# A new order for 1,687 hand-listed steps of an attention and expert kernel, fewer warm matmuls and one tiny activation

## The chip, the cores and the metric

The kernel runs on one core of a Trainium2 chip. The metric is device time in microseconds (us) of one execution, as the median of three runs. Its engines are TensorE (PE in the profile, its weight loads PEld), VectorE (DVE), ScalarE (ACT), GpSimd (POOL) and SyncE (SP), which here only issues transfers. Each works off its own queue in order, and semaphores tie them together.

## What is computed

Two stages follow each other: attention through 32 packed queries, in which softmax is taken twice, and then a feed-forward layer with a SiLU between two products.

```python
# q, k, v: (8, 8, 576, 64); p: (8, 8, 32, 64); w_in: (512, 2048); w_out: (2048, 512), all float32
def sm_attn(qq, kk, vv):
    s = scale * np.matmul(qq, kk.transpose(0, 1, 3, 2))
    a = np.exp(s - np.max(s, axis=-1, keepdims=True))
    return np.matmul(a / (np.sum(a, axis=-1, keepdims=True) + 1e-09), vv)
p_packed = sm_attn(p, k, v)
x = sm_attn(q, p_packed, p_packed)       # then (tokens, 512): 4608 x 512
h = x @ w_in
out = (h * (1.0 / (1.0 + np.exp(-h)))) @ w_out
```

## The kernel before

The program is a list of steps, `ORDER` (lines 56 to 123), that the last loop (lines 897 to 899) works off: a name, then numbers. Each step issues its instructions on one or two engines, and for TensorE, VectorE, ScalarE and SyncE an engine's queue is exactly the order in which the list names its steps. A queue that waits for a semaphore holds all behind it. So the list is the schedule, and a step late in one queue can hold three others.

The work falls into eight batches of 576 tokens, in two halves of 288 each. The steps that the text speaks of:

- Weights, in 20 chunks: `wf` loads a chunk (SP), `ws` scales (ACT), `wc`, `wz`, `wi` clip, sign and shift (DVE), `wj` joins (DVE, for some chunks POOL), `wu` and `wl` make an upper and a lower part (ACT, DVE). They split each float32 weight in two parts that TensorE multiplies at its faster float32 rate.
- Attention of batch b, `a` and a letter, then b and the half: `aS` or `as` scores (PE), `ac`/`aC` copies (ACT or DVE), `am`/`aM` maxima (DVE), `ax`/`aX` exponentials (ACT, the Exp table), `at` transposes (PE for batch 0, else DVE), `ay` spreads (for batches 1 to 7 small transfers issued by SP, line 383, eight for a half), `aa` the packed product (PE), `an`, `aj` scaling and copy (DVE) around `ai`, a transpose (PE), `aB` and `aU` transposes of batch 0 (PE), `aN`, `aD`, `aE`, `aV` differences, sums, shares and block transposes (DVE), `aH` and `aL` upper and lower part (ACT, DVE). `k`, `v`, `q` load a batch's inputs into two buffers that are used in turn.
- `pf`, `pp`, `pu`, `pl`: fetch a quarter of w_in, multiply it with the packed values (PE), and split the product (ACT, DVE).
- The feed-forward layer in units. Units 0 to 31 (batches 0 and 1): `h` (PE, line 611), `g` (ACT, the Silu table), `l` (DVE), `o` (PE, line 669). Units from 36 on: `B` (PE, line 611), `G` and `N` (ACT, Silu), `I` (three adds on POOL), `F` (ACT), `L` (DVE), `O` (PE, line 669). An `O` multiplies with sums of pairs of weights, which `S` loads (SP, line 740) into four buffers in turn. `E` and `Y` add up and store a half or the remaining rows (DVE, ACT, then SP).
- `r`, `R`, `ru`, `rl`, `rk`, `T` make and store those sums of weights during the first third.
- `W` (line 206) issues so many matmuls whose result nobody reads; `X0` and `X1` (line 187) are activations of one column, which make the compiler load the Exp or the Silu table there.

Two pairs of PSUM banks, `ps_two`, are used in turn by `W`, `h`, `B`, `pp` and the attention of batches 1 to 7 (line 200): a step that takes a pair waits until the readers of the step two turns earlier are done. All `W` steps share one pair that is taken once (lines 208 and 209), and the first two `pp` steps share another (lines 555 to 558).

Of the kernel before, what the change touches and what calls it, by code (L numbers as in the profile page):

```python
# [66 lines left out]
aH1.1 ac2.0 pl5 aL1.1 o6 o7 e7.0 r0 e7.1 h8 g8 ws13 l8 h9 g9 o8 ws14 wz12 wi12 wj12 as2.1 ac2.1 l9 am2 wc14 pp6 pu6  # L67
h10 pl6 g10 l10 X0 wc13 o9 v2 wz14 wi14 R0 h11 wz13 wi13 ax2.0 ax2.1 o10 g11 h12 wf15 wj13 l11 o11 at2.0 at2.1 wf17
ru0 rl0 rk0 ws15 ay2 g12 wc15 l12 h13 g13 h14 l13 pp7 o12 r1 pu7 g14 wz15 wj14 wi15 wu14 wj15 wu15 pl7 l14 wl15 o13
wl14 h16 wf16 ws17 wc17 q2 h15 g15 l15 R1 wz17 wi17 ru1 rl1 rk1 o14 o15 r2 g16 l16 e15.0 e15.1 ws16 h17 ar2 h18 g17  # L70
wj17 o16 h19 l17 wf18 g18 wc16 wz16 R2 ru2 l18 o17 wi16 wj16 pp8 rl2 r3 g19 pu8 l19 pl8 aa2 o18 h20 an2 X1 ai2 wf19
ws18 wc18 wz18 rk2 o19 wi18 aj2 g20 l20 aS2.1 x1 b0 aT2.1 wj18 pp9 ws19 wc19 x3 wu18 wl18 h21 pu9 pl9 g21 l21 x2 wz19
wi19 o20 h22 g22 l22 aM2.1 aN2.1 R3 h24 h23 wj19 wu19 wl19 ru3 rl3 rk3 X0 o21 r4 R4 o22 T0 T3 g23 l23 o23 g24 l24 h25
h26 e23.0 ru4 rl4 rk4 e23.1 g25 l25 r5 o24 pp10 g26 l26 aS2.0 o25 aT2.0 pu10 pl10 aX2.1 h27 aM2.0 aN2.0 aX2.0 aD2.0 X1
b1 aE2.0 T1 T2 h28 k3 o26 R5 ru5 rl5 rk5 T5 g27 l27 h29 T4 aV2.0 aH2.0 g28 r6 R6 l28 o27 g29 l29 o28 h31 aD2.1 aL2.0
h30 ru6 rl6 rk6 T6 r7 o29 g30 R7 l30 aE2.1 aV2.1 v3 g31 o30 aH2.1 ru7 X0 l31 rl7 o31 rk7 e31.0 e31.1 pp11 Z0. pp12 Z1.
F32 L32 O32 aL2.1 pf13 S36 pu11 T7 pl11 as3.1 pu12 F33 pl12 S37 as3.0 ac3.0 L33 O33 ac3.1 F34 am3 F35 ax3.0 B36 L34
G36 S39 I36 B37 G37 L35 N37 N36 O34 ax3.1 S38 pp13 pu13 O35 B38 pl13 pf14 at3.0 F36 I37 Y0 L36 F37 at3.1 G38 I38 L37
B39 N38 N39 ay3.0 O36 ar3 B40 G39 I39 F38 L38 pp14 pu14 q3 N40 O37 G40 O38 I40 B41 F39 L39 G41 pl14 F40 I41 L40 B42
G42 X1 O39 S40 O40 N41 F41 N42 ay3.1 B43 N43 I42 F42 L41 S41 aa3 G43 O41 X0 an3 L42 ai3 aj3 B44 S42 N44 G44 aS3.0 O42  # L80
B45 S44 I43 aT3.0 aM3.0 B46 F43 L43 I44 F44 N45 L44 G45 I45 S45 S43 aN3.0 O43 S46 pf15 E2.0 G46 F45 L45 N46 B47 O44
G47 N47 S47 pp15 I46 aS3.1 F46 L46 pu15 pl15 aT3.1 aX3.0 aD3.0 pf16 I47 O45 F47 O46 L47 B49 aE3.0 X1 k4 S49 N49 G49
S48 I49 B48 G48 pp16 pu16 aM3.1 O47 I48 N48 aN3.1 q4 F48 pl16 B50 F49 L48 L49 G50 I50 B51 N51 O48 N50 G51 I51 S51
as4.0 aX3.1 aV3.0 aD3.1 F50 S50 aH3.0 aL3.0 as4.1 pf17 X0 O49 ac4.0 ac4.1 B52 F51 L50 L51 S52 B53 G52 N52 am4 O50 N53
v4 pp17 pf18 O51 G53 aE3.1 aV3.1 aH3.1 B55 aL3.1 S53 pu17 S54 S55 pl17 I52 F52 L52 E2.1 ax4.0 ax4.1 I53 F53 L53 B54
N54 G54 I54 N55 O52 at4.0 O53 G55 I55 F54 B56 L54 B57 F55 X1 L55 N56 G57 I57 S57 at4.1 G56 N57 O54 pp18 pu18 pl18 O55
I56 F56 L56 ar4 B58 S56 O56 F57 L57 G58 B60 N58 B59 I58 F58 O57 ay4.0 L58 N60 G59 N59 G60 S58 O58 I59 F59 L59 I60
ay4.1 F60 S59 pf19 B61 N61 S60 G61 B62 I61 N62 S61 L60 O59 E3.0 G62 aa4 I62 F61 B63 N63 S62 L61 an4 G63 ai4 O60 aj4
aS4.0 aT4.0 aM4.0 pp19 aS4.1 F62 pu19 pl19 L62 aT4.1 I63 S63 O61 B64 N64 G64 I64 S64 aN4.0 B65 N65 F63 L63 aX4.0 B66
O62 O63 S66 pf20 G65 I65 aD4.0 aE4.0 S65 F64 F65 k5 L64 B67 O64 N66 L65 O65 G66 aV4.0 as5.0 aH4.0 G67 aL4.0 N67 I66  # L90
F66 L66 S67 aM4.1 pp20 X0 ac5.0 S72 as5.1 O66 I67 v5 F67 L67 pf21 O67 pu20 pl20 ac5.1 B72 aN4.1 F68 S73 L68 E3.1 X1
aX4.1 G72 B73 N73 I72 G73 am5 N72 O68 F69 L69 pp21 F70 pu21 aD4.1 q5 pl21 aE4.1 aV4.1 S74 B74 pf22 O69 L70 I73 N74 O70
F71 aH4.1 L71 O71 F72 L72 aL4.1 S76 Y2 F73 G74 ax5.0 L73 I74 B75 ax5.1 O72 N75 S75 ar5 O73 at5.0 B76 G75 B77 S77 F74
L74 I75 O74 G76 at5.1 F75 L75 I76 F76 G77 O75 N76 pp22 ay5.0 ay5.1 N77 pu22 L76 O76 I77 F77 S78 pf23 pl22 B78 N78 S79
B79 L77 G78 O77 N79 I78 aa5 F78 L78 O78 G79 I79 an5 F79 L79 S80 B80 G80 S82 B81 N80 G81 N81 I80 F80 B82 N82 I81 S81 k6
O79 L80 E4.0 ai5 G82 X0 I82 B83 S84 F81 O80 aj5 L81 N83 X1 G83 I83 aS5.0 aT5.0 pp23 aM5.0 pu23 pl23 aN5.0 pf24 X0
aS5.1 aT5.1 aX5.0 S83 O81 F82 L82 B85 F83 L83 aD5.0 N85 aM5.1 aE5.0 aV5.0 B84 G84 X1 N84 O82 G85 X0 aH5.0 I84 pp24
aN5.1 S85 aL5.0 pf25 pu24 pl24 I85 F84 O83 L84 aX5.1 aD5.1 aE5.1 F85 L85 B87 N87 G87 v6 B86 N86 S87 G86 O84 as6.0 S86
ac6.0 I87 pp25 pu25 pl25 pf26 I86 F86 as6.1 ac6.1 S88 O85 q6 L86 F87 L87 B88 G88 I88 N88 B89 G89 I89 S89 am6 O86 O87
B90 S90 S91 aV5.1 aH5.1 aL5.1 F88 L88 N89 E4.1 F89 L89 N90 G90 pp26 pu26 pl26 ax6.0 B91 ax6.1 at6.0 at6.1 ay6.0 O88  # L100
B92 O89 I90 N91 G91 S92 ar6 I91 X1 B93 X0 F90 L90 O90 S94 F91 N92 L91 G92 B94 O91 I92 G93 F92 N93 L92 N94 I93 O92 F93
L93 B95 G94 I94 S93 S95 F94 N95 B96 G95 I95 pf27 O93 L94 G96 I96 ay6.1 F95 L95 S96 N96 B97 G97 O94 F96 N97 O95 S97 aa6
L96 E5.0 an6 B98 G98 ai6 aj6 I97 N98 S98 O96 S100 aS6.0 S99 F97 L97 I98 F98 L98 k7 pp27 aT6.0 pu27 X1 pl27 O97 B99 G99
N99 B100 N100 G100 X0 B101 I99 F99 B102 aM6.0 aN6.0 aX6.0 N102 L99 G101 N101 pf28 I100 aD6.0 aE6.0 O98 O99 F100 L100
G102 aS6.1 aT6.1 pp28 aV6.0 I101 aM6.1 F101 pu28 I102 as7.0 pl28 aH6.0 aL6.0 O100 L101 F102 L102 B103 G103 I103 S101
O101 S102 ac7.0 as7.1 ac7.1 pf29 N103 F103 L103 S103 S109 pp29 pu29 pl29 v7 S108 O102 O103 am7 F104 B109 L104 B108
aN6.1 X1 X0 pf30 E5.1 X1 X0 aX6.1 aD6.1 F105 X1 L105 O104 O105 F106 G109 I109 F107 N108 aE6.1 L106 aV6.1 L107 O106 q7
O107 aH6.1 aL6.1 G108 I108 S111 S110 F108 L108 N109 F109 pp30 L109 Y4 pu30 ax7.0 ax7.1 B110 G110 I110 N110 pl30 at7.0
at7.1 ay7.0 O108 B111 G111 I111 O109 F110 N111 B113 N113 F111 B112 L110 S112 G112 O110 L111 O111 G113 S113 S114 I112
I113 F112 B115 L112 N112 F113 L113 B114 N115 G114 I114 S115 G115 O112 B116 N114 F114 B117 L114 ay7.1 S116 G116 N116  # L110
O113 I115 F115 O114 pf31 ar7 S117 N117 L115 aa7 I116 G117 B118 an7 ai7 aj7 F116 L116 S118 N118 O115 E6.0 G118 I117
# [831 lines left out]
```

## Time and profile before

| | us |
|---|---|
| median of three runs | 683.6 |
| lowest, highest | 683.32, 684.54 |
| the profiled execution | 684.45 |
| its span, first to last instruction | 682.7 |
| PE busy in it | 663.7 (97%) |
| DVE busy | 426.3 (62%) |
| ACT busy | 418.5 (61%) |
| POOL busy | 227.5 (33%) |

The execution has 14,810 instructions. A busy share over the whole span hides that the stages differ, so it is read by stage: for each stretch of time, how long each engine was busy. Where TensorE is idle, the timeline says what ended the wait. Matmuls overlap, so that their ends are modelled: the time from one start to the next says more than a duration.

### The profile page before, as it was taken

To read this page: it belongs to the slowest core of one execution; us is meant where nothing else is said; L and a number is where in the kernel's file an instruction comes from. 1 tells how busy PE (TensorE), PEld (TensorE's weight loads), DVE (VectorE), ACT (ScalarE), POOL (GpSimd) and SP (SyncE) were. 2 spreads that over 40 slices of the span, in tenths; PEclk is the share of its full clock that TensorE was granted. 3 is DMA by queue.
4 is the path that set the end of the run, shared out by engine and by line. 5 is a ranking of instruction groups with operands and counts; after the bars stand their busy time and mean duration, and the time that the engine had idled before them with its cause. 6 is when DMAs were issued, how large, how long until landed. Compare 5 with 4: busy or idle time off the path is not lost.

```text
span 682.7 us, 14810 instructions
## 1 busy us (share of the span) xinstructions
PE 663.7 (97%) x5980; PEld 586.4 (86%) x5980; DVE 426.3 (62%) x588; ACT 418.5 (61%) x702; POOL 227.5 (33%) x336
## 2 busy tenths in 40 slices
...
GB/s 359 320 150 334 156 172 167 331 346 209 258 291 334 188 303 329 334 321 264 253 343 343 127 277 292 362 274 270 330 284 372 75 262 294 246 249 262 167 172 46
DMA packets 55107, 178.62 MB, mean 262 GB/s; under 512 B 21760, under 2 KB 25856, under 8 KB 47360
## 3 DMA queue, kind: packets, MB, share of 16 engines
...
q8 instruction: 47, 0.77, 0.4%
q10 hardware_dynamic: 96, 0.13, 0.1%
q14 instruction: 20, 0.16, 0.1%
...
## 4 chain that ended last, share of the span: by engine, by line
PE 80%; DVE 10%; ACT 4%; issue 2%; SPq 2%; DMA 2%; POOL 1%; ACTq 0%; DVEq 0%
PE ps_acc L669 46%; PE ps_two L611 26%; PE ps_two L304 6%; PE ps_two L404 2%; SPq L383 1%; DVE win L281 1%; DVE w_raw L273 1%; DMA kvq_t<-in_pkT 1%; DVE g_lo L629 1%; DVE g_lo L663 1%; DVE w_raw L269 1%; ACT g_hi L659 1%; DVE win L285 1%; DVE o L811 1%; ACT g L633 0%
## 5 line engine op out<-in xcount | busy, mean ns | idle before, releaser
L663 DVE TENSOR_TENSOR g_lo<-g,g_hi 128x896 fp32r<-128x896 f32 x96 | 108.6, 1134 | 134.1 <-ACT g_hi L659 130.8
L669 PE MATMUL ps_acc<-wo_hi,g_lo 128*128 128x256 f32 (+1 forms) x576 | 182.1, 316 | 2.6 <-DVE g_lo L629 2.6
L669 PE MATMUL ps_acc<-wo_hi,g_hi 128*128 128x256 f32 (+1 forms) x576 | 182.7, 317 | 0.7 <-DVE o L811 0.7
L669 PE MATMUL ps_acc<-wo_lo,g_hi 128*128 128x256 f32 (+1 forms) x576 | 181.2, 315 | 0.0
L611 PE MATMUL ps_two<-a_hi,pw_hi 128*128 128x288 f32 x512 | 152.0, 297 | 1.8 <-DVE tm L331 1.1
L611 PE MATMUL ps_two<-a_hi,pw_lo 128*128 128x288 f32 x512 | 150.9, 295 | 0.0
L611 PE MATMUL ps_two<-a_lo,pw_hi 128*128 128x288 f32 x512 | 150.5, 294 | 0.3 <-DVE a_lo L542 0.3
L643 POOL TENSOR_TENSOR g<-g 128x128 f32<-128x128 f32 x96 | 51.0, 531 | 273.8 <-ACT g L633 241.9
L659 ACT CAST g_hi<-g 128x896 fp32r<-128x896 f32 x96 | 90.0, 941 | 76.7 <-POOL g L645 38.9
L669 PEld LDWEIGHTS ps_acc<-wo_hi,g_hi 128*128 128x128 f32 x576 | 108.1, 188 | 13.2 <-issue 5.4
L669 PEld LDWEIGHTS ps_acc<-wo_hi,g_lo 128*128 128x128 f32 x576 | 108.3, 188 | 11.9 <-DVE g_lo L629 4.2
L669 PE MATMUL ps_acc<-sums_of_w,g_hi 128*128 128x256 f32 x576 | 115.7, 282 | 0.1
L669 PEld LDWEIGHTS ps_acc<-wo_lo,g_hi 128*128 128x128 f32 x576 | 108.2, 188 | 6.5
L611 PEld LDWEIGHTS ps_two<-a_hi,pw_hi 128*128 128x128 f32 x512 | 96.3, 188 | 8.8 <-issue 2.3
L669 PEld LDWEIGHTS ps_acc<-sums_of_w,g_hi 128*128 128x128 f32 x576 | 87.8, 188 | 14.1 <-issue 12.3
L611 PEld LDWEIGHTS ps_two<-a_lo,pw_hi 128*128 128x128 f32 x512 | 96.4, 188 | 1.4 <-DVE a_lo L542 0.5
L611 PEld LDWEIGHTS ps_two<-a_hi,pw_lo 128*128 128x128 f32 x512 | 96.2, 188 | 0.0
L633 ACT ACTIVATE g<-ps_two 128x512 f32<-128x512 f32 x96 | 57.1, 598 | 42.7 <-PE ps_two L611 22.5
L669 PE MATMUL ps_acc<-sums_of_w,g_lo 128*128 128x256 f32 x288 | 80.0, 278 | 0.0
L644 POOL TENSOR_TENSOR g<-g 128x256 f32<-128x256 f32 x96 | 73.8, 770 | 6.5
L645 POOL TENSOR_TENSOR g<-g 128x128 f32<-128x128 f32 x96 | 56.7, 592 | 6.5
L669 PEld LDWEIGHTS ps_acc<-sums_of_w,g_lo 128*128 128x128 f32 x288 | 54.1, 188 | 0.4 <-DVE g_lo L663 0.2
(129 smaller groups left out, 835.9 us busy)
## 6 DMA issues: line engine op xcount, KB each, us to landing
sums_of_w<-sums_of_w SPq DMA_DIRECT2D x96, 768.0 KB, 6.4
...
sums_of_w<-w_sums SPq DMA_DIRECT2D x8, 768.0 KB, 4.5
```

The source lines that it names most:

```text
L269: nc.vector.tensor_scalar(up.bitcast(F32), up.bitcast(F32), TOP, -TOP, op0=ALU.min, op1=ALU.max)
L273: nc.vector.scalar_tensor_tensor(low, up, -(2**31), low, op0=ALU.bitwise_and, op1=ALU.bitwise_or)
L304: nc.tensor.matmul(bank(par)[NP * i : NP * i + NP], lhs(r, i), rhs(r, i), start=True, stop=True)
L404: nc.tensor.matmul(self.ps[NP * i : NP * i + NP, par * D : par * D + D], e, vs[:n, c, h * D : h * D + D], start=(c == 0), stop=(c == 4),)
L611: nc.tensor.matmul(bank, p[:, par, cols], a[:, par], start=(n == 0), stop=(n == len(todo) - 1))
L633: nc.scalar.activation(g[:, : 4 * P].rearrange("p (e s) -> p e s", e=2), made["h", u, None][..., :MAIN], AF.Silu)
L643: nc.gpsimd.tensor_tensor(x[:, 4], x[:, 0], x[:, 2], ALU.subtract)
L644: nc.gpsimd.tensor_tensor(x[:, 5:7], x[:, 0:5:4], one, ALU.subtract)
L645: nc.gpsimd.tensor_tensor(x[:, 7], x[:, 3], x[:, 6], ALU.add)
L659: nc.scalar.copy(both[0], g)
L663: nc.vector.tensor_tensor(g_lo, g, g_hi.bitcast(F32), ALU.subtract)
L669: nc.tensor.matmul(out, g[:, rows], w, start=(first and n == 0), stop=(last and n == 2), skip_group_check=True)
```

## The change

The list of steps is replaced by another one. It holds the same steps except that 39 warm matmuls remain of 50 and one tiny activation (`X1`, once) of 41. Almost every step stands elsewhere than before, within what the data allow. Each `W` step now takes a pair of banks of its own turn, and each `pp` step takes a whole pair, where the first two shared one. Nothing else in the program differs. Of the list the diff shows the first ten lines of both versions, and of the new one those later lines that the text speaks of.

```diff
@@ the order of steps (first tenth of each; all that follows is reordered too)
-wf0 W2 ws0 W2 k0 W2 wc0 W2 W1 W2 W2 wz0 wi0 as0.0 as0.1 am0.0 W1 W2 wf1 W2 ax0.0 am0.1 wf2 at0.0 ax0.1 ws1 ay0.0 ws2
-v0 ar0 W2 wf4 wc2 wz2 wc1 q0 wz1 at0.1 ay0.1 wi1 wf3 W2 W2 wf5 aa0 W1 an0 ws4 wf7 ai0 wi2 aj0 aS0.0 aC0.0 wj1 wj0 pp0
-wu1 pu0 wj2 wc4 W1 aB0.0 wz4 pl0 W1 W2 wi4 aM0.0 aN0.0 ws3 wl1 wf6 aS0.1 wj4 aC0.1 aB0.1 aM0.1 aX0.0 aD0.0 ws5 aN0.1
-pp1 pu1 W2 W2 W1 k1 aX0.1 aE0.0 wc3 aD0.1 W2 wc5 ws6 W2 W2 W2 W2 W2 W2 aE0.1 W2 X1 aU0.0 ws7 aH0.0 wz5 wz3 aU0.1 aH0.1
-wi5 pl1 as1.0 wf9 wi3 aL0.0 aL0.1 wj5 wj3 ac1.0 wu5 as1.1 h0.0 wu3 ac1.1 h0.1 g0.0 h1.0 g0.1 X0 wl5 wl3 am1 v1 wc6 wf8
-ax1.0 ax1.1 l0.0 l0.1 wz6 at1.0 at1.1 o0.1 wc7 wz7 g1.0 h1.1 g1.1 pp2 o0.0 pu2 ar1 pl2 h2.0 l1.0 l1.1 wi6 ws8 wi7 wj6
-g2.0 wc8 o1.1 l2.0 ws9 wf10 pp3 h2.1 wz8 wi8 wc9 wz9 g2.1 pu3 l2.1 pl3 X1 o1.0 wj7 wu7 wl7 ws10 o2.0 ay1 wj8 o2.1 wf11
-h3.0 g3.0 h3.1 q1 wi9 wj9 aa1 g3.1 wc10 wz10 l3.0 pp4 wi10 l3.1 pu4 ws11 wj10 an1 pl4 o3.0 wc11 wf12 ai1 aj1 o3.1 wz11
-h4 wu10 h5 g4 aS1.0 wl10 l4 o4 ws12 wi11 aT1.0 aM1.0 g5 aN1.0 wc12 aX1.0 l5 aS1.1 X0 X1 aT1.1 wf13 aD1.0 h6 g6 h7
-aM1.1 wj11 wu11 o5 k2 aE1.0 aV1.0 l6 pp5 aN1.1 wl11 aH1.0 g7 as2.0 l7 aX1.1 X0 aL1.0 aD1.1 pu5 wf14 aE1.1 x0 X1 aV1.1
...
+W1 W5 wf0 ws0 wc0 wz0 W4 wi0 k0 as0.0 as0.1 am0.0 W6 W1 wf1 am0.1 ax0.0 at0.0 ax0.1 wj0 ar0 ay0.0 at0.1 ws1 wc1 wz1
+ay0.1 v0 wf2 q0 wi1 aa0 an0 ai0 aj0 wf5 wj1 pp0 wf3 ws2 wc2 wz2 wi2 wj2 pu0 pl0 aS0.0 W1 aC0.0 aS0.1 wu1 aB0.0 wl1 ws5
+aC0.1 W1 wf6 aM0.0 wc5 aB0.1 aN0.0 ws3 aM0.1 aX0.0 wc3 aD0.0 ws6 aN0.1 aX0.1 W7 aE0.0 aU0.0 pp1 aD0.1 wz3 wf7 aE0.1
+wf4 ws7 aU0.1 aH0.0 k1 wi3 wz5 aL0.0 wj3 ws4 pu1 wc4 wc6 wu3 pl1 wi5 v1 as1.0 aH0.1 aL0.1 ac1.0 as1.1 ac1.1 h0.0 g0.0
+wl3 wj5 wu5 wz4 am1 wi4 h0.1 g0.1 wl5 wj4 wf9 W13 ax1.0 h1.0 h1.1 ax1.1 X1 wf8 l0.0 wc7 at1.0 l0.1 o0.1 g1.0 at1.1 pp2
+g1.1 wz7 wz6 l1.0 l1.1 o0.0 pu2 wi6 pl2 h2.0 wi7 h2.1 wj6 ws8 wc8 o1.1 wj7 g2.0 l2.0 wu7 ws9 wf10 ar1 wz8 wl7 g2.1 pp3
+pu3 wi8 wc9 l2.1 ws10 o1.0 o2.0 o2.1 wz9 pl3 h3.0 wi9 wj8 g3.0 h3.1 g3.1 ay1 wf11 aa1 wj9 wc10 pp4 pu4 l3.0 o3.0 an1
+wz10 ai1 l3.1 wi10 pl4 aj1 ws11 wc11 wz11 wj10 o3.1 wu10 q1 wl10 h4 g4 l4 h5 aS1.0 aT1.0 g5 wf12 wi11 aM1.0 aN1.0
+aX1.0 l5 o4 aS1.1 h6 aT1.1 aM1.1 aN1.1 x0 aD1.0 k2 wj11 wu11 wl11 aX1.1 g6 v2 o5 aE1.0 aV1.0 aH1.0 wf13 l6 h7 aD1.1 g7
+l7 ws12 aL1.0 wf14 pp5 pu5 aE1.1 aV1.1 o6 as2.0 o7 pl5 aH1.1 ac2.0 aL1.1 e7.0 h8 wc12 h9 e7.1 g8 x1 h10 l8 g9 wz12
...
+h11 o10 g11 l11 wi15 wc13 o11 g12 l12 h13 q2 wz13 o12 ax2.0 wi13 wj13 pp7 wj15 ax2.1 r1 wu15 wl15 g13 l13 wf16 at2.0
...
+S38 N37 I37 F37 pp13 B39 pu13 L37 I38 F38 O37 pf14 N39 G39 I39 L38 O38 F39 pl13 B40 N40 G40 B41 L39 S41 G41 I40 F40
...
+I41 pp14 S39 N41 O39 L40 O40 pu14 F41 pl14 B42 N42 B43 ay3.0 G42 ay3.1 S43 N43 I42 B44 N44 L41 O41 G43 F42 L42 aa3 S42
...
+aT3.0 I46 aM3.0 aN3.0 S47 F46 B47 G47 I47 O45 N47 aS3.1 pp15 S46 L46 aT3.1 aM3.1 O46 aX3.0 aN3.1 S48 pu15 F47 pl15
...
+O70 ax5.0 ax5.1 F71 ar5 L71 F72 L72 O71 Y2 pf22 at5.0 B75 I73 F73 G74 L73 O72 O73 G75 N75 I74 B76 I75 F74 at5.1 L74
...
+B96 L94 G95 I95 G96 S94 O93 F95 L95 ay6.0 ay6.1 B97 S96 O94 O95 I96 S97 G97 I97 N96 E5.0 F96 N97 aa6 L96 F97 an6 L97
...
+aN7.0 S118 B119 N119 B120 F118 O117 N120 G119 I119 F119 L118 O118 G120 L119 aX7.0 I120 F120 S119 B121 S121 N121 G121
...
+G124 I124 F124 L123 O123 E6.1 L124 aE7.1 N125 B127 G125 I125 F125 L125 B126 G126 G127 aV7.1 I126 N126 N127 O124 S125
...
+N135 I134 S134 F134 L134 N136 O134 G135 I135 G136 F135 S135 B137 L135 I136 F136 G137 I137 N137 L136 B138 G138 I138
...
+O135 F137 B139 S136 O136 L137 G139 I139 S138 S137 F138 O137 F139 L138 O138 L139 F140 L140 S139 O139 E7.1 F141 L141
...
 
     def keep_warm(n):
 
-        if "warm" not in made:
-            made["warm"] = two_banks()
+        ps = two_banks()
         for _ in range(n):
-            nc.tensor.matmul(made["warm"][:, 0, :P], ident, ident, start=True, stop=True)
+            nc.tensor.matmul(ps[:, 0, :P], ident, ident, start=True, stop=True)
 
     def load_k(b):
         t = in_turn(kvq, [P, 5 * DM], F32, "kvq_t")
@@ -552,13 +550,10 @@
             nc.sync.dma_start(t.rearrange("p f i n -> p (f i n)"), w_in32[self.f // FJ])
 
         def products(self):
-            if self.f != 1 or self.nf > 1:
-                made["pair_of_packs"] = two_banks()
-            at = P if self.nf == 1 and self.f == 1 else 0
-            self.ps = made["pair_of_packs"][:, :, at : at + self.nf * P]
+            self.ps = two_banks()
             w = made["quarter"] if self.f // FJ >= FROM_RING[self.b] else win[:, self.f : self.f + self.nf]
             heads(
-                lambda par: self.ps[:, par].rearrange("p (f n) -> p f n", n=P),
+                lambda par: self.ps[:, par, : self.nf * P].rearrange("p (f n) -> p f n", n=P),
                 made["packs", self.b],
                 lambda r, i: w[r, :, i].bitcast(F32),
             )
@@ -571,10 +566,10 @@
                 made["pw", b, j] = [t.rearrange("p (r n) -> p r n", r=2)[:, :, AT_PART : AT_PART + JW] for t in both]
             c = slice(self.f % FJ * P, (self.f % FJ + self.nf) * P)
             self.hi, self.lo = (t[:, :, c] for t in made["pw", b, j])
-            nc.scalar.copy(self.hi, self.ps)
+            nc.scalar.copy(self.hi, self.ps[:, :, : self.nf * P])
 
         def lower(self):
-            nc.vector.tensor_tensor(self.lo, self.ps, self.hi.bitcast(F32), ALU.subtract)
+            nc.vector.tensor_tensor(self.lo, self.ps[:, :, : self.nf * P], self.hi.bitcast(F32), ALU.subtract)
```

## Rows read from the trace of the kernel before

**Rows 1.** Busy time by stage: stretch, length, PE, PEld, DVE, ACT, POOL, granted clock, DMA share, GB/s.
```profile
0.00:20.00 20.00, 14.78 (x208) 11.76 (x209) 10.29 (x23) 9.33 (x18) 1.74 (x7) 0.99 0.93 366
20.00:40.00 20.00, 17.11 (x156) 12.99 (x157) 19.13 (x35) 15.50 (x32) 2.08 (x2) 0.92 0.64 249
40.00:61.00 21.00, 19.34 (x205) 14.51 (x204) 19.18 (x32) 16.64 (x34) 3.38 (x2) 1.00 0.62 227
61.00:140.00 79.00, 76.23 (x581) 61.46 (x580) 72.34 (x92) 60.05 (x97) 22.32 (x19) 1.00 0.63 229
140.00:660.00 520.00, 518.38 (x4735) 470.56 (x4734) 296.64 (x396) 310.56 (x514) 197.34 (x306) 1.00 0.74 274
660.00:683.00 23.00, 17.89 (x104) 15.15 (x102) 8.74 (x13) 6.39 (x11) 0.69 (x2) 0.98 0.10 34
```

**Rows 2.** Groups by line, whole span: count, busy us, mean ns, idle before.
```profile
L211 PE MATMUL ps_two<-ident 128*128 128x128 f32 x100 | 15.9, 320 | 1.4 <-POOL ident masks.py:199 1.4
...
L188 ACT ACT_TABLE_LOAD x27 | 34.6, 1283 | 1.2 <-PEq L935 0.7
...
L622 ACT ACT_TABLE_LOAD x3 | 3.8, 1283 | 0.0
```

**Rows 3.** Timeline of PE (start, us, what, idle before): aa0, aS0.0, h0.0, o4.
```profile
13.78 1.73 PE L404 MATMUL ps_acc<-kvq_t,tm 128*32 128x64 f32 x80 [0.30 <-DMA kvq_t<-in_v]
...
18.23 0.77 PE L304 MATMUL ps_acc<-rest,ppT 64*32 64x320 f32 x16 [1.08 <-DVE ppT L427]
...
33.81 0.40 PE L611 MATMUL ps_two<-a_hi,pw_hi 128*128 128x288 f32 x1 [0.35 <-ACT tm L331]
...
64.79 0.50 PE L669 MATMUL ps_acc<-wo_hi,g_hi 128*128 128x512 f32 x1
```

**Rows 4.** Timeline of DVE: an0, aj0, aM0.0, aE0.1, pl4.
```profile
16.49 0.28 DVE L414 TENSOR_TENSOR pp<-ps_acc,rd 128x128 f32<-128x128 f32 x1
...
17.90 0.28 DVE L427 COPY ppT<-ps_acc 128x128 f32<-128x128 f32 x1
...
21.49 0.96 DVE L488 TENSOR_REDUCE on_tokens<-ps_acc 128x24 f32<-128x768 f32 x1
...
30.13 0.68 DVE L526 TENSOR_TENSOR tm<-tm,on_tokens 128x512 f32<-128x512 f32 x1
...
59.15 1.23 DVE L577 TENSOR_TENSOR pw_lo<-ps_two,pw_hi 128x1024 fp32r<-128x1024 f32 x1
```

**Rows 5.** Timeline of SP, issue of transfers: wf2, v0, ay1.
```profile
2.61 0.60 SPq L258 DMA_DIRECT2D w_raw<-in_w_in  x1
3.25 0.45 SPq L236 DMA_DIRECT2D kvq_t<-in_v  x1
...
42.24 10.42 SPq L383 DMA_DIRECT2D tm<-tm  x16
```

**Rows 6.** Busy time by stage again, short stretches (clock third from the end).
```profile
16.00:18.00 2.00, 0.33 (x1) 0.14 (x1) 1.97 (x5) 0.18 (x1) 1.04 (x1) 1.00 1.03 418
...
20.00:23.00 3.00, 3.00 (x20) 2.66 (x28) 2.65 (x5) 1.85 (x4) 0.00 (x0) 0.50 1.07 444
```

**Rows 7.** Timelines of ACT and PE around step ac5.0 and the scores behind it.
```profile
352.12 1.28 ACT L188 ACT_TABLE_LOAD   x1
353.42 0.20 ACT L188 ACTIVATE ident<-ident 128x1 f32<-128x1 f32 x1
...
354.20 0.72 PE L304 MATMUL ps_two<-kvq_t 64*32 64x288 f32 x16 [0.43 <-ACT tm L331]
```

**Rows 8.** DVE's timeline at step wi13; waits from 98 to 104 us (total, times, longest).
```profile
98.21 2.39 DVE L281 TENSOR_SCALAR win<-w_raw 128x1024 int32<-128x1024 int32 x1
...
PE ps_acc L669 <- DVE g_lo L629: 1.2, 1, 1.2
```

**Rows 9.** Transfers by line: count, KB each, median us from issue to landing.
```profile
sums_of_w<-sums_of_w SPq DMA_DIRECT2D x96, 768.0 KB, 6.4
...
tm<-tm SPq DMA_DIRECT2D x56, 40.0 KB, 2.0
```

100 lines of the change are left out of this document (44 added, 56 removed).

## The prediction

> **What bounds the kernel now.** I read the stages first. From 140 to 660 us TensorE is busy 518.4 of 520 us, from 61 to 140 us 76.2 of 79, but in the first 61 us only 14.8 + 17.1 + 19.3 = 51.2 of 61, and part of that is warm-up matmuls that compute nothing [rows 1]. So TensorE sets the end, and what an order can win lies in the start, plus 2.8 + 1.6 = 4.4 us of idle TensorE between 61 and 660 us. The last 23 us hold 5.1 us of idle time (a wait on E7.1 and the tail behind the last matmul), and both orders end in the same steps, so I count nothing there. In the start VectorE is the engine that is never free: 19.1 of 20 us from 20 to 40, 19.2 of 21 from 40 to 61, 72.3 of 79 after that [rows 1]. The start is thus a question of how soon VectorE gets the steps of batch 0's attention done between the weight chunks, and of what TensorE waits for behind them.
>
> **What doesn't change.** By step names the two orders hold the same work, but for two things. The warm matmuls go from 50 to 39: the trace has 100 instructions for 50 [rows 2], so 22 fewer; at 0.11 us from one to the next when dense that is 2.4 us less TensorE work, nearly all of it in idle places before. And of 41 tiny activations one is left. Counting the changes between Exp and Silu along ScalarE's queue gives 62 table loads before (as in the trace, six groups, the first of 27, the last of 3 [rows 2]) and 38 after: 24 x 1.283 + 40 x 0.20 [rows 7] = 39 us less ScalarE work. ScalarE is busy 310.6 of 520 us in the long stage [rows 1], so this is no bound; I cost it at nothing by itself, since TensorE covers it. Where the cover is missing a load costs up to its 1.28 us: at 352 us one stands just ahead of the copy ac5.0, and TensorE sat idle 0.43 us for that copy [rows 7]. After the change a load comes right ahead of the first activation that needs it (g0.0, ax1.0), and those two are counted below.
>
> The Trainium skill ("ScalarE: Activation LUTs", What ACT_TABLE_LOAD costs) gives about 2.66 us for a switch, 1283 ns of load and the rest drain. The trace agrees with the load alone: the activation behind one that ends at 353.40 starts at 353.42 [rows 7]. By the page's sum each of the two loads in the start would add 1.4 us, and the start would win some 1.5 us less.
>
> **The start, step by step.** I follow the new queues with durations of the old trace. Nothing differs up to am0.1.
> - v0 is now issued ahead of wf2 rather than behind it and lands about 1.2 us sooner (half a MB at the 0.42 MB/us of the loading stage [rows 6]; order of issue [rows 5]). aa0, which waited for v0 at 13.78 [rows 3], starts about 13.0 with ay0.0 done at 12.9, and ends at 14.7.
> - Behind it VectorE stands ready: an0 follows at once, at 14.75, where before it came at 16.49 behind wc1, wz1, wi1 [rows 4]. aj0 comes right behind ai0 and ends at 15.7, where before it ended at 18.2 [rows 4]. So aS0.0 starts at 16.2 in place of 18.23 [rows 3]; its part of q0 is there (loads in order: about 15.2).
> - aS0.1 now precedes aB0.0. ws5 and wu1 stand on ScalarE ahead of aC0.1, which gives back a little: aM0.0 at 19.4 against 21.49. aM0.0, aN0.0, aM0.1, aD0.0, aN0.1, aE0.0, aD0.1, wz3, aE0.1 then follow densely to 27.9; before, aE0.1 ended at 30.8 [rows 4].
> - aU0.1 28.0 to 29.1. Packs 0 and 1 now take one pair of banks each, so as1.1 waits for pl1, the reader of pp1: TensorE idles from 29.75 to 30.8. h0.0 starts at 31.5, against 33.81 [rows 3].
> - g0.0 carries a table load (31.4 to 32.6), ax1.0 the next (34.7 to 36.0). W13 (2.9 us of TensorE) lies between h0.1 and h1.0; it is hidden, since o0.1 waits for l0.1 until about 38.8, behind am1, wi4, wl5, wj4 and at1.0 on VectorE.
> - From there VectorE is dense: pl2 ends at 42.1, l2.1 at 48.6. ay1's sixteen small DMAs hold SP's queue for 10.4 us [rows 5]; they start at 39.5 instead of 42.24, so aa1 has its data at 51.7, just when TensorE comes to it. an1, wz10, l3.1, wi10, pl4 follow: pl4 ends at 58.0 (59.15 + 1.23 before [rows 4]), h4 starts then, and o4 at 61.8. Before, o4 started at 64.79 [rows 3].
>
> TensorE has the same real work behind it at o4 in both orders, so the start gains **3.0 us**. Bounds: 4.5 if W13 and the two loads cost nothing anywhere, 1.0 if VectorE loses 2 us to things the walk leaves out (an add of GpSimd beside it stretches a step, as wi13's 2.39 us show [rows 8]).
>
> **61 to 660 us.** TensorE's time for each kind of step and for each change of kind is the same in both orders (B to O 46 and 51 times, O to O 25 and 19, packs to O 12 and 13): under 0.3 us either way, taken as nothing. Of the 4.4 us of idle time two examples show the kinds. At 98 to 102 us wi13 and wj13 stood on VectorE ahead of l11, and o11 waited 1.2 us [rows 8]; the new order has wi13 and wj13 well behind l11. And the tiny activations' loads [rows 7] are gone. I take half of it, **-2.2 us** (bounds 0 and -4.4).
>
> Against this stand new waits. From B to its O the new order leaves a mean of 10.9 us of TensorE work, the old 11.3; the smallest is 5.0 in the new one (unit 40) and 5.6 in the old (unit 78), where the chain G, I, F, L takes about 5. Pairs of banks that come free with only 1.0 us of TensorE work between are fewer (7 and 11). But loads are later: with 1.9 us fixed and 0.39 MB/us (estimates from the small copies [rows 9] and [rows 6]) and each load issued when the slot or the queue ahead of it frees, the old order has no load with less than 1.0 us to spare in this stage, the new one eleven (S38, S39, S46, S118, S125, S134, pf22, pf34, ay6.1 among them), most behind a store of results or of spreads on SP's queue. I take **+1.2 us** (0 to 7.6, which is what these eleven fall short of 1.0 us together); nearer to the low end, because the median landing of 6.4 us [rows 9] holds queueing that such a lone late load doesn't meet.
>
> **The sum.** -3.0 - 2.2 + 1.2 = -4.0 us. The profiled execution took 684.45 us, its span 682.7; the median of the three runs, 683.6, is 0.85 below it. So 680.4 by the profiled one, and **679.6 us** as a median.
>
> **The rivals.**
> - *The start's gain stays, the rest is a draw or eats it.* New waits cancel the idle time saved and 1 to 3 us more: 682 to 683.6 us. For it: eleven loads with little to spare, where there was none. Against: TensorE idles only 1.6 of 520 us [rows 1] in an order with covers nearly as thin. Chance 0.16.
> - *VectorE takes the start's gain back.* If it is the bound up to 140 us, an earlier o4 wins nothing, as VectorE's work is the same. For it: 72.3 of 79 us busy. Against: 6.7 us idle there, and at o8 to o17 my running sums of the two engines leave VectorE 1 to 3 us ahead in the new order. It would leave 682.5 us. Chance 0.08.
> - *The clock falls.* Before, TensorE did 0.33 us of work from 16 to 18 us and the granted clock was then 0.50 from 20 to 23 us, the 1.2 GHz level [rows 6]. In the new order the warm matmuls are fewer, and TensorE has nothing from about 22.4 to 25.6. At half clock aU0, as1 and h0 cost 0.5 to 1.7 us more, most of it under VectorE's dense queue: 680.1 to 681.3 us. Chance 0.18. The Trainium skill ("TensorE: Matmul & The Clock Gate", HAM oscillation) says that a stretch without matmuls sends the array back to half rate, so that each burst behind it starts cold; rows 6 agree with it, and by it this rival is the likely one in the start.
> - *Slower: SP's queue.* SP issues in order, so one store that waits for its result (E2.0, E6.0, E6.1, E7.0, Y0, Y2) holds the loads of sums and packs behind it. If landings are 1 us later than I take them, the eleven loads cost up to 7.6 us, and with -3.0 and -2.2 the kernel takes 686.0 us; it decides from about 0.7 us of lateness on average. For it: the count above; against: no load cost TensorE time before at a cover of 1.0 us. Chance 0.15.
>
> **How the numbers follow.** Forecast 0.43, with the clock rival 0.18 beside it, both faster by over 0.2% (1.4 us, about what a measurement of this kernel can tell from no change); the draw 0.16 and VectorE 0.08 lie half on either side of that bound; SP's queue 0.15 is slower. That gives faster 0.72, within 0.2% 0.13, slower 0.15. The range goes from 675.8 (start -4.5, three quarters of the idle time, -3.3, and no new wait) to 685.0, which leaves out the worst of the slower case.
>
> **What would show it.** Right: aj0 ends near 15.7, h0.0 starts near 31.5, o4 near 61.8 us; ScalarE busy about 380 us with 38 loads; from 140 us on, idle TensorE of 1 to 3 us. Wrong: o4 later than 63.5 us, a second or longer stretch at the 0.50 clock, or waits of TensorE for sums_of_w, w_quarter or tm by DMA, which the old trace doesn't have.

## The result and the profile after

The changed kernel takes **690.9 us** (median of 4 runs, 690.35 to 693.71) against 683.5 for the kernel before beside it: a ratio of 1.0114, 95% interval 1.0091 to 1.0137. Forecast were 679.6 us and a range up to 685.0. The profiled execution took 690.36 us, its span 688.6, so it stands 5.9 us behind the one of before (684.45, span 682.7). The medians stand 7.4 us apart: the profiled execution of before was 1.0 us above its median here, the changed kernel's 0.5 below. What follows compares the two profiled executions.

Busy time by stage, the same columns and stretches as [rows 1]:

```profile
0.00:20.00 20.00, 14.54 (x215) 10.65 (x215) 11.38 (x26) 10.67 (x21) 1.74 (x7) 1.00 0.92 370
20.00:40.00 20.00, 17.89 (x134) 14.01 (x134) 18.23 (x35) 16.73 (x34) 2.46 (x2) 0.74 0.77 307
40.00:61.00 21.00, 20.96 (x221) 16.51 (x219) 20.08 (x33) 16.67 (x33) 3.31 (x2) 1.00 0.57 181
61.00:140.00 79.00, 75.90 (x573) 60.26 (x572) 73.42 (x90) 54.28 (x85) 23.02 (x19) 1.00 0.66 245
140.00:660.00 520.00, 513.85 (x4666) 465.14 (x4665) 295.10 (x394) 277.46 (x458) 198.62 (x301) 1.00 0.72 269
```

From 40 to 61 us TensorE is hardly idle any more (20.96 of 21 us, before 19.34 [rows 1]). From 140 to 660 us it is idle 6.15 us where it was idle 1.62. So the start was won and the long stage was lost.

What TensorE waited for (total us, times, longest), the first lines of its waits:

```profile
PE ps_acc L664 <- DMA sums_of_w<-sums_of_w: 3.6, 5, 1.2
PE ps_two L302 <- DMA w_quarter<-w_in: 2.2, 1, 2.2
PE ps_acc L474 <- DVE tm L524: 2.0, 2, 1.3
```

The two transfers in front are new: before, TensorE waited for neither. That is 5.8 us of waits for loads. (The lines of the program have moved: L664 was L669, L302 was L304.)

I then set the two traces beside each other by the names of the steps. The table has the start of a step against its start before, in us (negative is earlier):

| step | h0.0 | o4 | o31 | O35 | O51 | O103 | O143 (last) |
|---|---|---|---|---|---|---|---|
| start before | 33.8 | 64.8 | 195.6 | 214.2 | 287.9 | 516.1 | 675.8 |
| after | -2.52 | -2.99 | -2.07 | -1.61 | +0.43 | +5.37 | +5.89 |

The start gave 2.99 us, 0.9 of it went again by o31, and **7.96 us were lost behind o31**. The timelines show the start. First TensorE's rows for aS0.0, h0.0 and o4, then VectorE's for aj0, aM0.0, aE0.1 and pl4, which answer to [rows 3, 4]:

```profile
15.39 0.75 PE L302 MATMUL ps_acc<-rest,ppT 64*32 64x320 f32 x16
...
31.29 0.61 PE L606 MATMUL ps_two<-a_hi,pw_hi 128*128 128x288 f32 x1
...
61.80 0.50 PE L664 MATMUL ps_acc<-wo_hi,g_hi 128*128 128x512 f32 x1
```

```profile
14.81 0.29 DVE L425 COPY ppT<-ps_acc 128x128 f32<-128x128 f32 x1 [0.42 <-PE ps_acc L421]
...
18.22 0.95 DVE L486 TENSOR_REDUCE on_tokens<-ps_acc 128x24 f32<-128x768 f32 x1
...
26.62 0.68 DVE L524 TENSOR_TENSOR tm<-tm,on_tokens 128x512 f32<-128x512 f32 x1
...
56.47 1.22 DVE L572 TENSOR_TENSOR pw_lo<-ps_two,pw_hi 128x1024 fp32r<-128x1024 f32 x1
```

The largest loss comes next: SP's issues around step Y2, whose four stores (64 KB each) stand ahead of pf22's load of 1 MB; TensorE's wait at pp22 and what follows; and busy time with the granted clock (third from the end) in three short stretches.

```profile
377.90 1.75 SPq L799 DMA_DIRECT2D out<-o  x4
379.70 0.42 SPq L550 DMA_DIRECT2D w_quarter<-w_in  x1
```

```profile
387.22 1.09 PE L302 MATMUL ps_two<-w_quarter,ppT 64*32 64x512 f32 x16 [2.16 <-DMA w_quarter<-w_in]
...
388.70 0.41 PE L664 MATMUL ps_acc<-wo_hi,g_hi 128*128 128x256 f32 x1
388.91 0.41 PE L664 MATMUL ps_acc<-wo_lo,g_hi 128*128 128x256 f32 x1
```

```profile
384.00:388.00 4.00, 1.84 (x25) 1.04 (x23) 0.00 (x0) 0.71 (x2) 1.88 (x4) 1.00 0.94 381
388.00:389.00 1.00, 1.00 (x13) 0.76 (x6) 0.00 (x0) 0.60 (x1) 0.00 (x0) 0.85 0.22 92
389.00:392.00 3.00, 3.00 (x16) 3.00 (x16) 2.22 (x2) 1.25 (x2) 0.00 (x0) 0.50 0.03 12
```

The buffer for pf22 was free at 360.5 us (the end of pp21, the last reader of what it held). Its load stood in SP's queue behind stores that waited for their results until 377.9, so it was issued at 379.70, landed at 387.1, and TensorE waited 2.16 us for it. Behind that wait the granted clock was 0.50, the 1.2 GHz level, until 392.1 us, with matmuls 0.21 us apart where they are 0.11 apart at the full clock: 1.6 us more. Five other loads went the same way. In the table, "issued" is when SP issued the load and "landed" when its data was there. The excess is the time from one TensorE step to the next, less the shortest such time for that pair of kinds of steps in the two traces:

| load | issued, landed | step that waited | excess, us |
|---|---|---|---|
| S36 | 203.7, 216.3 | O36 | 1.06 |
| S38 (behind Y0's stores) | 218.5, 224.6 | O38 | 0.56 |
| S39 (behind S41) | 224.4, 232.2 | O39 | 0.70 |
| pf22 (behind Y2) | 379.7, 387.1 | pp22, and the clock behind it | 2.35 + 1.61 |
| S92 (behind pf27) | 463.4, 472.3 | O92 | 1.38 |
| S118 (behind E6.0's store) | 576.5, 584.7 | O118 | 0.65 |

These come to 8.3 us. The excess of all steps behind 200 us is 19 to 20 us after (it depends on how finely the kinds are told apart) and some 11.5 before, about 8 us more, as the starts of the steps say. S46 (behind E2.0) landed 0.3 us and S134 (behind E7.0) 0.1 us before its use, and neither cost anything in this execution.

### The profile page after: what moved, and what is told of

Same layout as the page of the kernel before. It is cut to its first block, busy times and chain, and to the rows that moved or that the text cites. A ratio compares the mean times of both kernels' runs of the same rounds, so it can differ in the third digit from the quotient of the medians.

```text
span 688.6 us, 14712 instructions
## 1 busy us (share of the span) xinstructions
PE 666.9 (97%) x5958; PEld 587.8 (85%) x5958; DVE 427.7 (62%) x588; ACT 382.9 (56%) x638; POOL 232.4 (34%) x336
## 4 chain that ended last, share of the span: by engine, by line
PE 76%; DMA 8%; DVE 7%; ACT 4%; issue 2%; SPq 1%; POOL 1%; DVEq 0%; ACTq 0%
PE ps_acc L664 44%; PE ps_two L606 23%; PE ps_two L302 6%; DMA sums_of_w<-sums_of_w 5%; DMA win<-in_w_out 2%; PE ps_two L402 2%; DVE g_lo L624 1%; DMA w_quarter<-w_in 1%; DVE w_raw L271 1%; DVE w_pair L742 1%; DVE o L806 0%; ACT g_hi L618 0%; ACT g L617 0%; DVE w_raw L267 0%; PE ps_two L209 0%
## 5 line engine op out<-in xcount | busy, mean ns | idle before, releaser
L664 PE MATMUL ps_acc<-wo_hi,g_hi 128*128 128x256 f32 (+1 forms) x576 | 183.5, 319 | 0.8 <-DVE o L806 0.8
L664 PE MATMUL ps_acc<-wo_hi,g_lo 128*128 128x256 f32 (+1 forms) x576 | 182.5, 317 | 0.0
L664 PE MATMUL ps_acc<-wo_lo,g_hi 128*128 128x256 f32 (+1 forms) x576 | 182.0, 316 | 0.0
L638 POOL TENSOR_TENSOR g<-g 128x128 f32<-128x128 f32 x96 | 52.3, 545 | 277.3 <-ACT g L628 277.0
L664 PE MATMUL ps_acc<-sums_of_w,g_hi 128*128 128x256 f32 x576 | 116.7, 284 | 3.6 <-DMA sums_of_w<-sums_of_w 3.6
L664 PEld LDWEIGHTS ps_acc<-wo_hi,g_hi 128*128 128x128 f32 x576 | 108.6, 189 | 13.3 <-issue 5.2
L664 PEld LDWEIGHTS ps_acc<-wo_hi,g_lo 128*128 128x128 f32 x576 | 108.8, 189 | 8.7 <-DVE g_lo L624 0.9
L664 PEld LDWEIGHTS ps_acc<-wo_lo,g_hi 128*128 128x128 f32 x576 | 108.7, 189 | 6.5 <-DVE wo_lo L295 0.2
L664 PEld LDWEIGHTS ps_acc<-sums_of_w,g_hi 128*128 128x128 f32 x576 | 88.5, 189 | 18.2 <-issue 9.4
L664 PE MATMUL ps_acc<-sums_of_w,g_lo 128*128 128x256 f32 x288 | 80.3, 279 | 0.3 <-DVE g_lo L658 0.3
L639 POOL TENSOR_TENSOR g<-g 128x256 f32<-128x256 f32 x96 | 72.2, 755 | 6.3
L640 POOL TENSOR_TENSOR g<-g 128x128 f32<-128x128 f32 x96 | 61.3, 640 | 6.3
L664 PEld LDWEIGHTS ps_acc<-sums_of_w,g_lo 128*128 128x128 f32 x288 | 54.5, 189 | 0.5 <-DVE g_lo L658 0.5
```

Source lines behind the costliest of these rows:

```text
L638: nc.gpsimd.tensor_tensor(x[:, 4], x[:, 0], x[:, 2], ALU.subtract)
L639: nc.gpsimd.tensor_tensor(x[:, 5:7], x[:, 0:5:4], one, ALU.subtract)
L640: nc.gpsimd.tensor_tensor(x[:, 7], x[:, 3], x[:, 6], ALU.add)
L664: nc.tensor.matmul(out, g[:, rows], w, start=(first and n == 0), stop=(last and n == 2), skip_group_check=True)
```

## The experiments

Each experiment's ratio and 95% interval are against runs of the kernel before that were taken beside it (medians 683.9 to 684.4 us). The theory after the result: **the loss is loads of sums and of packs that stand too late in SP's queue**, each behind a store that waits or behind another load. The rivals: the rest of the new order is slower by itself (its mix of steps, its pairs of banks); the start's changes (clock, warm matmuls) do damage that shows later; the tiny activations that were dropped were worth something.

**Each half alone.** Two hybrids, cut at step Z1. (198 us): the new order up to there and the old one behind it, and the other way round. Steps that the first part had not yet done follow at the cut. (The lines marked - and + here tell an order in words; further down, ... stands for steps left out.)

```diff
-  ORDER: new up to Z1., new behind
+  h1_new_start_old_rest: new up to Z1., then aH2.0 aL2.0 T6 v3, then the old rest
+  h2_old_start_new_rest: old up to Z1., F32 pu11 pu12 and the new rest
```

> The new order up to the step that opens the second stage (Z1., some 200 us), then the remaining steps in the old order (four steps that the new order hadn't done by then come first). Theory A, the loss lies in the later order alone, in loads that land late: at the last early unit the changed kernel was 2.07 us ahead, so 683.5 - 2.1 = 681.4 us. Rival B, the loss is made by the start (banks taken by each warm step, fewer table loads placed ahead, more half-clock time) and only shows later: 688 us or more. Rival C, the two stages don't fit at the seam: 684 to 686 us.

> The old order up to the same step, then the remaining steps in the new order. Theory A: the whole loss of the second stage stays, 7.96 us between the last early unit and the end, so 683.5 + 8.0 = 691.5 us, less the 1.2 us that a stretch of half clock cost at 388 us if that does not come back. Rival B: about 684 us.

Measured: h1 686.8 us, 1.0043 [1.0030, 1.0057]; h2 689.8 us, 1.0080 [1.0063, 1.0096]. In the traces, against before:

| step | o4 | o31 | O35 | O51 | O103 | O143 |
|---|---|---|---|---|---|---|
| h1 (new start) | -3.25 | -2.31 | +2.11 | +2.11 | +2.33 | +2.33 |
| h2 (new rest) | -0.86 | -0.78 | -0.32 | +2.02 | +3.40 | +3.47 |

h1's time fits none of the three prices (681.4, 684 to 686, 688 or more), and the trace has to tell. It has the start's gain, loses 4.4 us at the cut, and then the old rest loses 0.2 us. The loss at the cut is the hybrid's own: on VectorE, aL2.0 stands ahead of L32 there and waits 2.24 us for ScalarE, O32 waits 2.53 us, and the granted clock is then 0.50 from 202.3 to 205.8 us. TensorE's row for O32 and VectorE's rows there:

```profile
201.25 0.50 PE L665 MATMUL ps_acc<-wo_hi,g_lo 128*128 128x512 f32 x1 [2.53 <-DVE g_lo L659]
```

```profile
199.84 0.76 DVE L541 TENSOR_TENSOR a_lo<-tm,a_hi 128x576 fp32r<-128x576 f32 x1 [2.24 <-ACT a_hi L537]
200.51 0.68 DVE L659 TENSOR_TENSOR g_lo<-rest,g_hi 128x512 fp32r<-128x512 f32 x1
```

h2 loses 4.3 us behind o31 in its profiled run (687.9 us, the lowest of its four; no stretch at half clock behind the start), with S39, S92, S46, S134, S38 and pf22 landing 0.04 to 0.14 us ahead of their steps. Its start is the old one, so the -0.86 at o4 is a difference between two executions of the same steps; it bears on the start's gain below. TensorE's first wait there is the one of after:

```profile
PE ps_acc L668 <- DMA sums_of_w<-sums_of_w: 3.7, 5, 1.5
```

So the new rest loses time without the new start.

**The cut three units later,** to be rid of that loss, once with and once without the old rest's 29 tiny activations.

```diff
-  h1: new up to Z1., then the old rest
+  h3_seam_later: new up to O33 (S36 ahead of S37), then the old rest
+  h4_seam_later_no_tiny: h3 without the 29 steps X0, X1 of that rest
```

> The new order up to O33, with S36 ahead of S37 as in the old one, then the old order. The run before it lost 4.4 us between O32 and O35, at its seam alone (L32 stood behind aH2.0 and aL2.0 there); this seam keeps the new order's own steps around O32. Theory A (the later order's late loads are the loss, the start is a gain): 684.2 - 2.1 = 682 us, on the fast side of the kernel before. Rival B (the new start costs time later on whatever follows): 685 us or more.

> The same without the 29 tiny activations of the old rest: 16 fewer table loads, the others come right ahead of the first activation that needs them. If loads placed ahead are of use, each one moved into a path costs up to 1.28 us and the kernel takes 1 to 4 us more than the one before it; if ScalarE's time is what counts, it takes 0.5 to 2 us less; if TensorE covers either, the same within 0.5 us.

Measured: 691.5 us, 1.0104 [1.0085, 1.0123], and 691.3 us, 1.0103 [1.0088, 1.0118]. The later cut is worse, not better: o31 stands at -2.12, O35 already at +4.16, for TensorE waits there for ScalarE, which comes to its copies late at this seam, and the granted clock is 0.50 from 215.1 to 221.9 us; then O51 +5.76, O143 +6.83. Its longest wait in h3:

```profile
PE ps_two L303 <- ACT rest L633: 5.3, 1, 5.3
```

As a test of the start this hybrid failed. Two things can be kept: from O51 on the old rest loses about 1 us in 390, and the tiny activations of that rest are worth nothing that these runs show (0.1 us between the two medians, four runs each).

**One load.** The new order with pf22 ahead of Y2, nothing else.

```diff
-O70 ax5.0 ax5.1 F71 ar5 L71 F72 L72 O71 Y2 pf22 at5.0 B75
+O70 ax5.0 ax5.1 F71 ar5 L71 F72 L72 O71 pf22 Y2 at5.0 B75
```

> The changed kernel with a single step moved: the fetch pf22 stands just ahead of the store step Y2 in SP's queue, where it stood behind it. Nothing moves on any other engine. Theory A: the fetch is issued before the wait for Y2's result, lands some 8 us sooner, the 2.2 us wait at 385 us goes and with it the half clock behind it (1.2 us): 690.9 - 3.4 = 687.5 us. Rival D, the data path itself is the limit there (the transfers are slow whenever they are issued): 690 to 691 us.

Measured: 688.7 us, 1.0078 [1.0043, 1.0114]. In the trace pp22's wait and the half clock behind it are gone (3.96 us of the table above), and the other five waits for sums, 3.9 us, are still there. The median moved by 2.2 us only, and with five runs from 686.9 to 694.2 us its interval overlaps the changed kernel's. The two profiled executions differ by as little (690.36 and 688.24): this one's start was slower by 0.6 us at o4, with half clock at other places, and O134 now waited 1.25 us for S134. So the trace shows that this wait is gone, and the time alone does not settle its worth.

**All late loads.** The new order with eight loads issued earlier, and pf27 later so that it lets S92 and S95 go ahead; no other step moved.

```diff
-... pl11 S37 pl12 ...            aL2.0 B36 G36 S36 ...
+... pl11 S36 S37 pl12 ...        aL2.0 B36 G36 ...
-... am3 S40 ax3.0 ...            Y0 O36 G38 S38 N37 ...
+... am3 S40 S38 ax3.0 ...        Y0 O36 G38 N37 ...
-... L39 S41 ... pp14 S39 ...     E2.0 ... aN3.0 S47 ... pp15 S46 ...
+... L39 S39 S41 ... pp14 ...     S47 S46 E2.0 ...
-... S75 O70 ... Y2 pf22 ...      O91 pf27 S92 O92 at6.0 at6.1 S95 ...
+... S75 pf22 O70 ... Y2 ...      O91 S92 O92 at6.0 at6.1 S95 pf27 ...
-... S117 G116 ... aN7.0 S118 ... O131 E7.0 ... I134 S134 ...
+... S117 S118 G116 ... aN7.0 ... O131 S134 E7.0 ... I134 ...
```

> The changed kernel with nine steps moved that exist in SP's queue alone: S36, S38, S39, S46, S118, S134 and pf22 stand ahead of the store or load that held them, S47 goes with S46, and pf27 goes behind S92. Theory A: the waits of TensorE for loads go, which by starts of steps come to 1.06 + 0.56 + 0.70 + 2.35 + 1.61 + 1.38 + 0.65 = 8.3 us: 690.9 - 8.0 = 683 us, down to 681.5 if nothing else is lost behind 200 us. Rival D: 690 us. Rival E, half of what is won at one load is lost at the next (each load moved forward pushes another back): 686 to 688 us.

Measured: **682.9 us, 0.9982 [0.9973, 0.9991]**, 8 us less than the changed kernel (9 by the two ratios) and a little under the kernel before. The step starts against before: o4 -2.92, o31 -1.38, O51 -1.05, O103 -0.92, O143 -1.43: flat behind o31. The excess behind 200 us is 11 to 12 us (before some 11.5). Busy time of e2 by stage, SP's issue of pf22 with Y2's stores now behind it, and TensorE's row for pp22, which has no wait:

```profile
61.00:140.00 79.00, 75.92 (x574) 60.31 (x572) 72.21 (x90) 54.33 (x85) 23.04 (x19) 1.00 0.66 241
140.00:660.00 520.00, 518.66 (x4728) 470.43 (x4727) 298.76 (x396) 280.20 (x461) 202.60 (x306) 1.00 0.74 272
```

```profile
367.45 0.44 SPq L550 DMA_DIRECT2D w_quarter<-w_in  x1
376.35 1.73 SPq L799 DMA_DIRECT2D out<-o  x4
```

```profile
383.43 1.09 PE L302 MATMUL ps_two<-w_quarter,ppT 64*32 64x512 f32 x16
```

The load took longer than in the changed kernel (13.2 us, with five larger loads on their way at its issue, where the changed kernel had four small stores and the end of one load) and was still in time, since it was issued 12.2 us sooner. TensorE is busy 518.66 of 520 us, as before. This settles the cause: nine steps moved in SP's queue alone take the loss away, and the rest of the new order, left as it is, costs nothing by its mix and its banks that can be seen.

**The clock in the start.** e2's profiled run had 13.65 us at the 0.50 clock, from 21.1 us on. Six more warm matmuls there:

```diff
-aD0.0 ws6 aN0.1 aX0.1 W7 aE0.0 aU0.0 pp1 aD0.1
+aD0.0 ws6 aN0.1 aX0.1 W13 aE0.0 aU0.0 pp1 aD0.1
```

> The kernel with the loads moved earlier, and its warm step W7 ahead of aU0.0 made W13, on the same pair of banks: a test of the half-clock stretch (13.7 us of it from 21 us in the last run, 3.4 in the kernel before). If half clock costs the start what the rival of the prediction says, 0.5 to 1.7 us: 681.5 to 682.4 us, and fewer us at half clock. If VectorE covers it: 682.9 us whatever the clock. If the warm matmuls themselves hold up aU0.0 at half clock: 683.5 to 685 us.

Measured: 681.9 us, 0.9965 [0.9952, 0.9978]. The half clock lasted 6.8 us, h0.0 came at -2.94 instead of -2.76, o4 at -3.15 instead of -2.92, O143 at -2.51. The two intervals (e2's reaches down to 0.9973) overlap a little, so the 1.0 us between the medians is likely and not certain. That it is the clock's is not shown: of e4's five runs the one with a granted clock of 1.0 took longest (682.58 us), and e2's ten runs lie within 1.1 us of each other at granted clocks from 0.989 to 0.995.

**Two more waits, and a table load taken off its activation.**

```diff
-pp6 pu6 wc14 wz14 wf15 pl6 as2.1          O37 pf14 N39 ... L39 S39 S41
+pp6 pu6 pl6 wc14 wz14 wf15 as2.1          O37 S39 pf14 N39 ... L39 S41
 e6_load_ahead only, on top of that:
-aL0.0 wj3 ws4 pu1 wc4
+aL0.0 wj3 ws4 X1 pu1 wc4
```

> The order of e4_warmer_start (681.9 us) with two steps moved. pl6, which reads the pair of banks that h12 then waits for at about 92 us, goes ahead of wc14 and wz14 on VectorE's queue (h12 waited 1.3 to 1.5 us for it); S39 goes ahead of pf14 in SP's queue, since two loads of 768 KB issued together land one after the other. If both waits end last on the path (theory: TensorE is the bound there, so what it doesn't wait for is won), 680.5 to 681.0 us. Rival: VectorE is the bound up to 140 us, so that h12's wait only moves to a later step: 681.6 to 682.1 us, no change.

> e5_two_more with one tiny activation more, in the start: X1 right behind ws4, so that the Silu table is loaded about 1 us before g0.0 needs it and not by g0.0 itself. Theory that the tiny activations of the old start were worth something by the table load that they take off a chain (e3_old_no_tiny lost 1.7 us of median, all of it before o8): 0.3 to 1.0 us less than e5_two_more. Rival: the load lies on no chain here, as VectorE's queue ahead of l0.0 ends later: the same within 0.3 us, or 0.4 us more, when it delays pu1 and pl1.

Measured: e5 681.6 us, 0.9961 [0.9946, 0.9976]; e6 682.3 us, 0.9978 [0.9966, 0.9989]. The excess between o9 and h12 (some 1.5 us in e4) turned into 0.74 between h12 and h11 and 0.43 between o11 and h13 in e5, and the kernel is not measurably faster than e4: the rival holds, VectorE passes most of the wait on. In e6's trace the load ahead delayed pu1 and what follows: h1.0 came 1.2 us later than in e5, and the steps up to o12 0.8 to 0.9 us later; by o31 0.1 us of it was left. The two intervals overlap, so the runs show no gain by that load and no sure loss.

**What the old tiny activations were worth.** The old order without any, and with only the first seven (those ahead of o8).

```diff
-  before: 41 steps X0, X1
+  e3_old_no_tiny: none
+  e7_old_tiny_early: only the seven ahead of o8
```

> The old kernel with its 41 tiny activations left out and nothing else: one part of the change alone. 18 fewer table loads and 41 fewer activations, 31 us less ScalarE work. Priced at nothing in the prediction: 684.2 us, within 0.7. If the tiny activations hide a load where TensorE has no cover: 686 us or more. If they stand in the way (as at 352 us): 682.5 us.

> The old order with only those seven of its 41 tiny activations that stand ahead of o8; the 34 later ones are left out. If all that the tiny activations are worth lies in the start (in the trace of e3_old_no_tiny the whole loss was there, h4 2.0 us late, o8 3.1, then flat): 684.0 to 684.6 us, that is, the old kernel's time within 0.3. Rival: the later ones are worth something too (the load ahead of ac5.0 showed a wait of 0.43 us): 685 to 686.2 us.

Measured: e3 686.2 us, 1.0027 [1.0018, 1.0037]; e7 684.4 us, 1.0009 [1.0000, 1.0019]. So the old order lost 1.7 us without them, and about two thirds of that comes back with the first seven; in e3's trace all is lost by o8 (h4 +2.03, o8 +3.09, O143 +3.13). That trace is the longest of its nine runs (687.6 us), with 10.2 us at the 0.50 clock ahead of 61 us, where e7's had none and the one of before 3.4; e3's six runs at granted clocks of 0.997 and more took 685.3 to 686.3. Below are ScalarE's rows for g0.0 in e3, where the load now comes just ahead of the activation, and TensorE's longest wait from 31 to 61 us, which was 1.3 us before:

```profile
35.91 1.28 ACT L620 ACT_TABLE_LOAD   x1
37.21 0.38 ACT L620 ACTIVATE g<-ps_two 128x256 f32<-128x256 f32 x1
```

```profile
PE ps_two L302 <- ACT rest L622: 2.1, 1, 2.1
```

The load's 1.28 us stand between h0.0 and the packs behind it, and h1.0 is 1.1 us later against h0.0 than in e7's trace. But h0.0 itself, ahead of that load, is 1.3 us later than e7's. So the load is a part of the loss, and how the 1.7 us divide between loads and clock stays open. The new order lost nothing visible by dropping them, as its start walked as forecast; no run puts them all back there.

## Why the prediction was wrong, point by point

**What bounds the kernel** was read rightly: TensorE sets the end behind 61 us, and what an order can win lies in the start. It also held in the bad sense: the waits of TensorE behind 200 us (some 8 us of excess) went into the time (7.96 us).

**The start, -3.0.** Right in its steps: aj0 ends at 15.10 (forecast 15.7), aM0.0 starts at 18.22 (19.4), aE0.1 ends at 27.30 (27.9), h0.0 starts at 31.29 (31.5), pl4 ends at 57.68 (58.0), o4 starts at 61.80 (61.8). In size it is right against the one trace of before, and that trace was a late one: h2 and e7, which have the same steps up to o4, start it at 63.94 and 63.66 where the trace of before has 64.79, while six traces of the new start have 61.55 to 62.44. By these the start is worth some 2.2 us (an estimate from the means). The forecast took 3.0 us off a median that lies 0.85 us below the profiled execution, and so probably counted that late start twice. The rival that VectorE takes it back was a third right: 0.9 us of the 2.99 were gone by o31 (1.5 in e2's run), and e5 shows a wait on VectorE moving on.

**Idle time removed, -2.2.** Not found. The excess from 61 to 200 us was 5 to 6 us before and is about 1 us more after; behind 200 us it was some 11.5 before and is as much in e2, where the loads are in time. The waits that I named went, and others of the same size took their places: behind o9 at 88.9 us (h12 waits, some 1.5 us) and behind h7 (pp5 waits, some 0.8).

**New waits, +1.2: the step that failed.** I had found the late loads and given a price of 0 to 7.6 us; they cost 8.3 us (7.96 by the step starts). Four of the six waiting loads were among the nine that I named: S38, S39, S118 and pf22, and S134 in e1's run. S36 and S92, which cost 2.4 us, were not, and S125 and pf34, which were, landed 1 us ahead. The size of the term failed by the time that a late load takes to land: at the landing times that I assumed none of the six would have been waited for. They took 6.1 to 12.6 us, 2.2 to 8.7 us more than assumed, and the waits were 0.6 to 2.4 us. What I had wrong is the reason for taking the low end, that a lone late load would not meet the queueing in the median landing of 6.4 us [rows 9]. A late load is not alone: it is late because the queue was held, and what was held with it leaves with it (the six had two to six others on their way at their issue). I had also set its landing at 1.9 us and 0.39 MB/us, 3.9 us for 768 KB and 4.5 for 1 MB. Sorted by how many other transfers (the small spreads left out) were on their way at the issue, the loads of sums behind 200 us took (median us, and their number before):

| others on their way | 0 | 1 | 2 | 3 | 4 or more |
|---|---|---|---|---|---|
| before, loads | 10 | 25 | 28 | 24 | 9 |
| before | 4.5 | 5.7 | 6.3 | 8.2 | 10.6 |
| after | 4.4 | 5.3 | 6.8 | 8.3 | 10.0 |

Only 10 of 96 loads were lone in the trace of before, and even those took 0.6 us more than my 3.9. This table could have been made from the trace of before. By it S36, issued with six others on their way, takes 10 us or more (12.6). It is a rough guide: in the trace of before the loads with one to three others range from 4.1 to 10.7 us, and small transfers seem to count for less. pf22 had five others on their way, but four were stores of 64 KB and the fifth a load that was nearly done; it took 7.4 us, not 10, with two more loads issued behind it. I have not redone the price of all eleven loads with the table. The Trainium skill ("DMA: Bandwidth & Descriptors", Queues, rings and completion order) says that each DMA engine takes what one queue gave it in the order of its ring; the trace agrees: S36 and the six transfers ahead of it landed in the order of their issue, from 203.8 to 216.3 us.

**The rival "SP's queue"** (0.15, 686.0 us) is what happened: landings 1 us and more later than I took them, at its price of 7.6. It gave 686.0 rather than 690.9 because it kept the -2.2 of idle time (0 in fact), the 0.9 of the start that was lost, and 0.4 of the loads (7.96, 1.6 of it the clock behind pf22's wait); the last 1.4 us come with the medians, which lie 1.5 us further apart than the two profiled executions. My argument against it, that no load cost time before at a cover of 1.0 us, was about covers of 1.0 us and more by my own sum. By the trace two loads of the old order landed less than 1.0 us ahead of their use (S78 0.13, S92 0.61) and cost at most 0.16 us, so the old order had loads with less than I said, but too few to speak for or against a whole list of them.

**The rival "the clock falls"** came true as an event and not as a price: 10.2 us at the 0.50 clock between 20 and 34 us (before 3.4), with o4 where the forecast had it. e4 puts at most 1 us on it, and its own runs don't bear that out. Where the lower clock did cost was behind pp22, where I had not looked for it.

**ScalarE and the tiny activations.** Its busy time is 382.9 us (forecast 380) with 38 loads (forecast 38). Costing the dropped ones at nothing fits the new order's start; e3 shows it would have been wrong by 1.7 us for the old one. The activation behind a load starts 0.02 us after it (35.91 + 1.28, then 37.21 in e3), and ScalarE was not idle just ahead of the load, so it was right to leave out the longer switch that the prediction quotes.

**What it adds to:** -2.99 (start) + 0.92 (given back by o31) + 7.96 (loads) = +5.89 us, where -3.0 - 2.2 + 1.2 stood, all against the profiled execution of before. The kernel without its late loads, e2, is at 682.9 us, inside the range and 3.3 us above the forecast; e4 and e5, at 681.9 and 681.6, beat both kernels.
